# Fixed order of the first loads, b1 loaded as rows, and 40 unread transpositions ahead of TensorE's first work

## The chip, the cores and the metric

The kernel runs on one core of one Trainium2 chip. A core has five engines that each work through their own list of instructions in order: TensorE (PE, matmuls and transpositions through PSUM), VectorE (DVE), ScalarE (ACT), GpSimd (POOL) and SyncE (SP), which here only issues DMA transfers. They wait for each other and for transfers on semaphores. The metric is the device time of one execution in microseconds (us), less is better; a verdict compares medians of repeated runs.

## The reference

The program computes one layer and all its gradients. x is 2048 rows of 512. It is normalised over its rows (mean and variance), and two branches read the result: a recurrent attention with 32 heads of 128 over 64 segments of 32 rows, each preceded by 8 memory rows that the segment before has left, and an MLP with 1792 hidden units:

```python
def _B_ref(x, w1, b1, w2, b2):
    h = jnp.einsum('bsd,df->bsf', x, w1) + b1
    zero = jnp.zeros_like(h)
    r = jnp.where(h > zero, h, zero)
    h = r * r
    out = jnp.einsum('bsf,fd->bsd', h, w2) + b2
    return out
...
return x + _A_ref(xn, A_mem0, A_Wq, A_Wk, A_Wv, A_Wo, A_seg_len) + _B_ref(xn, B_w1, B_b1, B_w2, B_b2)
```

The outputs are that sum and the gradients of x, of the memory, of the four attention weights, and of w1, b1, w2, b2 for a given gradient grad_out. All inputs and outputs are bf16.

## The kernel before

The program runs stage after stage: the MLP forward together with the first half of its backward, the attention forward, the attention backward, and the weight gradients. The change touches only the start of the first stage, whose MLP matmuls the profile has up to about 220 us.

**Tiling of the first stage.** The 2048 rows are taken in eight blocks g of 256 rows. For each block, `ln(g)` normalises: ACT sums each half of the block (L1054), DVE subtracts the mean (L1059), ACT sums the squares (L1062), DVE scales (L1069), TensorE turns the result by 128 x 128 transpositions against an identity tile `ident` (L688), and DVE copies the turned block from PSUM to SBUF (L1078; the tile is PA for even blocks and xT for odd ones). `mlp_a(g)` multiplies W1 with the turned x and W2T with the turned gradient for 14 chunks of 128 hidden units (L1092, each chunk two groups of four matmuls), ACT adds b1 and applies the ReLU (L1095), DVE squares it and forms the hidden gradient (L1097, L1099), and a DVE sum over the turned gradient block gives a part of the gradient of b2 (`gb2p`, L1102). `mlp_b(g)` multiplies by W2 and by W1T.

**What has to be in place before block 0.** x block 0 (tile xN) and gradient block 0 (tile gxb, turned by TensorE into PB) come by DMA. The later gradient blocks come through a DMA that transposes (L1042, into gTb for odd blocks, PB for even ones). W1 and W2 come in four pieces each, of 4, 4, 4 and 2 chunks of 128 hidden units. W1 lies in the tile WB, W2 in a tile of its own (W in the profile). W2T and W1T are made from them by TensorE, two chunks at a time: eight transpositions into one PSUM bank, then one copy by DVE or ACT (L692, L694); that is called a turn here. b1 comes as a tile of 128 x 14 elements, b2 as one row.

**What sets the order.** Each piece of work is given to a planner with its cost, its reads and writes and, for a DMA, a time to landing. When all is given, `run()` simulates the engines and emits the instructions in the order in which the simulation has started them, by readiness and by rank (the longest chain behind a piece, plus `lift`). Once emitted, each engine keeps that order, whatever happens on the chip. The eleven large first loads, b1 and b2 were given like any other work, so the planner chose their order. That order on the SyncE queue is: W2 piece 3, a W2 piece, x block 0, a W2 piece, W1 piece 3, a W2 piece, gradient block 0, two W1 pieces, x block 1, the last W1 piece, b1, b2, the transposing load of gradient block 1, x block 2, then the first stores of normalised x (S_XN). The completion semaphores of this queue are eight that are used in turn, so that each transfer waits for the one eight places before it.

**PSUM.** The stage has two rings of four banks, "h" for the hidden chunks and "B" for the turns and the block outputs.

Of the kernel before, what the change touches and what calls it, by code (L numbers as in the profile page):

```python
# [15 lines left out]
BF16 = mybir.dt.bfloat16  # L16
F32 = mybir.dt.float32
P = 128
# [545 lines left out]
def kernel(  # L564
# [27 lines left out]
    nc = tc.nc  # L592
# [15 lines left out]
    FC = F // P  # L608
# [3 lines left out]
    xflat = A_x.flatten_outer_dims()  # L612
    gflat = grad_out.flatten_outer_dims()
# [56 lines left out]
    ident = const.tile([P, P], BF16, name="ident")  # L670
# [15 lines left out]
    def transpose_to(ps_ap, in_ap, base=0):  # L686
        k = in_ap.shape[0]
        nc.tensor.transpose(ps_ap, in_ap, ident[base:base + k, base:base + k])  # L688

    def ev(e, out, in_):  # L690
        if e == "v":
            nc.vector.tensor_copy(out, in_)  # L692
        elif e == "s":
            nc.scalar.copy(out, in_)  # L694
        else:
            nc.any.tensor_copy(out, in_)
# [22 lines left out]
    T_DMA = 0.42  # L719
# [273 lines left out]
    with tc.tile_pool(name="p0", bufs=1) as p0, \  # L993
# [4 lines left out]
        def tl(name, shape, dt=BF16):  # L998
            return p0.tile(shape, dt, name=name)

        W1 = WB[:, 0:DC * F].rearrange("p (c f) -> p c f", c=DC)
        W2T = WB[:, DC * F:2 * DC * F].rearrange("p (c f) -> p c f", c=DC)
        W2 = tl("W2", [P, FC, D])
        W1T = tl("W1T", [P, FC, D])
        b1Tb, b1T = tl("b1Tb", [P, FC]), tl("b1T", [P, FC], F32)
        b2r = tl("b2r", [1, D])
        ones_row = tl("ones_row", [1, P])
        nc.vector.memset(ones_row[:], 1.0)
# [5 lines left out]
        xN = [tl("xN%d" % z, [P, 2, D]) for z in range(3)]  # L1014
# [12 lines left out]
        gxb = [tl("gxb", [P, D], F32)] * 2  # L1027
        gN0 = gxb[0][:].bitcast(BF16).rearrange("p (c d) -> p c d", c=2)
        CUT = ((0, 4), (4, 8), (8, 12), (12, FC))
# [5 lines left out]
        sg = Stage(plan, {"h": (pp, 4), "B": (pp, 4)})  # L1035
        A = plan.add
        V = nc.vector
        R2 = lambda t, g: t[g * RB:(g + 1) * RB]
        pair = lambda t, g: R2(t, g).rearrange("(c p) d -> p c d", p=P)
# [4 lines left out]
        def ln_in(g, eng="SP"):  # L1044
            z = g % 3
            sg.dma(lambda: xN[z][:], lambda: pair(xflat, g), [], [("xN", z)], lat=3.5, eng=eng)

        def ln(g):
            z = g % 3
# [83 lines left out]
        def turn_w(u, nm):  # L1133
            bk = sg.bank("B", [P, 8, P], BF16, "ps_" + nm)
            src = W1 if nm == "W1T" else W2

            def tr(e):
                for f in range(2):
                    for dc in range(DC):
                        if nm == "W1T":  # L1140
                            transpose_to(bk()[:, DC * f + dc, :], W1[:, dc, (2 * u + f) * P:(2 * u + f + 1) * P])
                        else:
                            transpose_to(bk()[:, 2 * dc + f, :], W2[:, 2 * u + f, dc * P:(dc + 1) * P])
            A({"PE": 0.5}, tr, [(nm[:2], u // 2)], [bk.key])
            if nm == "W1T":
                out, in_ = W1T[:, 2 * u:2 * u + 2, :].rearrange("p f d -> p (f d)"), lambda: bk()[:].rearrange("p k r -> p (k r)")
            else:
                out, in_ = W2T[:, :, 2 * P * u:2 * P * (u + 1)], lambda: bk()[:].rearrange("p (c f) r -> p c (f r)", c=DC)
            A({"DVE": 0.8, "ACT": 1.1}, lambda e: ev({"DVE": "v", "ACT": "s"}[e], out, in_()), [bk.key], [(nm, u)])
# [27 lines left out]

        for g in range(NRB):
            if g == 0:
                ln_in(0)  # L1180
                for h, (f0, f1) in enumerate(CUT):
                    sg.dma(lambda f0=f0, f1=f1: W1[:, :, P * f0:P * f1],
                           lambda f0=f0, f1=f1: B_w1.rearrange("(c p) f -> p c f", p=P)[:, :, P * f0:P * f1], [], [("W1", h)], lat=4.5 + 3.0 * h)
                    if h == 0:
                        sg.dma(lambda: gN0, lambda: pair(gflat, 0), [], ["gxb"], lat=6.0)
                        sg.dma(lambda: b1Tb[:], lambda: B_b1.rearrange("(c p) -> p c", p=P), [], ["b1Tb"], lat=5.0)
                    sg.dma(lambda f0=f0, f1=f1: W2[:, f0:f1, :],
                           lambda f0=f0, f1=f1: B_w2.rearrange("(c p) d -> p c d", p=P)[:, f0:f1, :], [], [("W2", h)], lat=6.0 + 3.0 * h)
                sg.dma(lambda: b2r[:], lambda: B_b2.rearrange("(o n) -> o n", o=1), [], ["b2r"], lat=5.0)
                A({"DVE": 0.1}, lambda e: V.tensor_copy(b1T[:], b1Tb[:]), ["b1Tb"], ["b1T"])  # L1190
                ln(0)
                bk = sg.bank("B", [P, DC, RB], BF16, "ps_gT")

                def trg(e, bk=bk):
                    for k in range(2):
                        for dc in range(DC):
                            transpose_to(bk()[:, dc, k * P:(k + 1) * P], gN0[:, k, dc * P:(dc + 1) * P])
                A({"PE": 0.5}, trg, ["gxb"], [bk.key])
                A({"DVE": 0.7, "ACT": 1.05}, lambda e, bk=bk: ev({"DVE": "v", "ACT": "s"}[e], gTb[0], bk()[:]), [bk.key], [("gT", 0)])
                for u in range(FC // 2):  # L1200
                    turn_w(u, "W2T")
                ln_in(1)
                ln_in(2)
                ln(1)
            if g == 0:
                mlp_a(0)
                for u in range(FC // 2):
                    turn_w(u, "W1T")
            if g:
                mlp_a(g)  # L1210
            if g == NRB - 1:
                first_in()
            mlp_b(g)
            if g + 2 < NRB:
                ln(g + 2)
            if g + 3 < NRB:
                ln_in(g + 3)
            if g < 6:
                for h in range(2):
                    x = 2 * g + h  # L1220
                    t, dc = x // DC, x % DC
                    Wsrc = (A_Wq, A_Wk, A_Wv)[t]
                    fc = 4 + 6 * h
                    A({"POOL": 0.15}, lambda e, t=t, dc=dc, g=g, fc=fc: nc.gpsimd.tensor_copy(
                        Wqkv[t][0:1, dc, 0:1], aT[g % 2][0:1, fc, 0:1]), [("aT", g % 2, fc)], [("Wg", x)])
                    sg.dma(lambda t=t, dc=dc: Wqkv[t][:, dc, :],
                           lambda Wsrc=Wsrc, dc=dc: Wsrc[dc * P:(dc + 1) * P].rearrange("p h e -> p (h e)"),
                           [("Wg", x)], [], lat=8.0, cost=0.6, eng="POOL")
        for i in range(NI):
# [5 lines left out]
                   lat=8.0, cost=0.6, eng="POOL")  # L1235
        plan.run()

    with tc.tile_pool(name="fw", bufs=1) as fw, \
# [33 lines left out]
        for g in range(JQ):  # L1272
            h = g // 2
# [12 lines left out]
        sg = Stage(plan, {"c": (0, 4), "f": (4, 2), "m": (6, 2)}, pc.tile([P, 8, 512], F32, name="ps"), 0.9)  # L1286
        A = plan.add
        V = nc.vector
# [302 lines left out]
    if True:  # L1591
# [42 lines left out]
        sg = Stage(plan, {"c": (0, 5), "r": (5, 1), "f": (6, 2)}, pc.tile([P, 8, 512], F32, name="ps"), 1.8)  # L1634
        A = plan.add
        V = nc.vector
# [325 lines left out]
    with tc.tile_pool(name="p5b", bufs=1) as p5b, tc.tile_pool(name="p5e", bufs=1) as cs1, \  # L1962
# [142 lines left out]
```

## Time and profile before

| what | us |
|---|---|
| median of 3 runs | 2854.03 |
| lowest and highest of them | 2837.7 and 2859.14 |
| the profiled execution | 2858.51 |
| its span | 2856.7 |
| TensorE busy in the span | 2688.5 (94%) |
| VectorE busy | 1611.3 (56%) |
| ScalarE busy | 1189.5 (42%) |

Times in the profile are us from the span's start. The page has the busy time of each engine; other views of the same trace list instructions by time, with the idle time ahead of an instruction and what ended it in brackets, or the busy time of every engine in chosen stretches. PEld is TensorE's weight load, which lies beside its matmuls; SPq is the SyncE queue. Matmuls are pipelined, so for TensorE the distance from start to start says more than a duration.

### The profile page before, as it was taken

The numbers are of one execution on the slowest core, as the hardware profiler recorded it, in microseconds if no ns is written. First come the engines' busy times: TensorE is split into PE (matmuls) and PEld (weight loads), VectorE is DVE, ScalarE is ACT, GpSimd is POOL, SyncE is SP. The second block draws the span as 40 slices with busy tenths as digits, with TensorE's granted clock in tenths as the row PEclk, the third lists the DMA queues.
The fourth block names the chain that finished last, engine by engine and source line by source line (L and its number), as shares of the span: only waits on it lengthen the run. The fifth ranks groups of instructions, "written<-read, shape, count | busy, mean of one in ns | idle before, by whom it ended". The sixth has DMA issues, their size and how long they took to land. (4 is left out here: it accounts for less than half of the span.)

```text
span 2856.7 us, 113933 instructions
## 1 busy us (share of the span) xinstructions
PE 2688.5 (94%) x47469; PEld 1556.2 (54%) x47640; DVE 1611.3 (56%) x4769; ACT 1189.5 (42%) x2781; POOL 939.8 (33%) x2630
## 2 busy tenths in 40 slices
PE   8998999999999999789999999999999899999999
PEld 6664565555656555565555555555555444444444
DVE  5645667666666667566566666666666602232322
ACT  4333455455545555455555555555555400000000
POOL 1102223222322223344455554545454301111111
PEclk9999999999999999999999999999999999999999
DMA  6657768777777765368889898888888799788861
GB/s 195 213 170 200 199 196 215 207 199 200 207 203 210 200 187 165 118 149 216 221 230 240 226 236 235 232 224 232 221 233 214 207 358 298 229 255 266 253 185 43
DMA packets 557595, 606.26 MB, mean 212 GB/s; under 512 B 229925, under 2 KB 358454, under 8 KB 555030
## 3 DMA queue, kind: packets, MB, share of 16 engines
q1 hardware_dynamic: 541654, 544.09, 69.0%
q0 software_dynamic: 15424, 54.87, 5.7%
q8 instruction: 374, 6.13, 1.0%
q14 instruction: 143, 1.17, 0.2%
HBM read 290.14 MB, written 272.12 MB: 197 GB/s over the span
## 5 line engine op out<-in xcount | busy, mean ns | idle before, releaser
L802 PE MATMUL ps<-WA,PA 128*32 128x512 bf16 x6144 | 366.8, 379 | 5.5 <-DVE PA L1490 3.7
L2042 PE MATMUL ps<-WA,WB 128*128 128x512 bf16 x1505 | 330.7, 379 | 2.2 <-DVE gwo L692 0.6
L802 PEld LDWEIGHTS <-PA 128*32 128x32 bf16 x8192 | 207.3, 96 | 202.5 <-issue 12.2
L2042 PEld LDWEIGHTS <-WB 128*128 128x128 bf16 x1896 | 185.5, 98 | 224.4 <-issue 0.9
L692 DVE CAST gwo<-ps 128x512 bf16<-128x512 f32 x64 | 40.0, 683 | 398.9 <-PE ps L2042 267.2
L1660 PE MATMUL ps<-WA,dT 128*32 128x512 bf16 x4096 | 248.2, 382 | 9.7 <-DVE dT L785 8.0
L694 ACT CAST dN<-ps 128x512 bf16<-128x512 f32 x356 | 206.0, 586 | 108.9 <-PE ps L912 77.3
L694 ACT CAST gwo<-ps 128x512 bf16<-128x512 f32 x64 | 33.1, 599 | 517.2 <-PE ps L2042 357.9
L928 POOL COPY BDA<-PB 32x128 bf16<-32x128 bf16 x287 | 82.6, 288 | 413.8 <-DVE PLp L1458 266.8
L2053 POOL DMA_DIRECT2D out_dram<-gwo x96 | 71.3, 751 | 294.2 <-ACT gwo L694 263.4
L1660 PEld LDWEIGHTS <-dT 128*32 128x32 bf16 x4096 | 94.2, 97 | 125.8 <-DVE dT L785 46.8
L785 DVE STREAM_TRANSPOSE dT<-dN 128x256 f32<-128x256 f32 x256 | 109.4, 434 | 68.3 <-ACT dN L694 65.8
L934 POOL COPY BDL<-dSL 32x64 bf16<-32x64 bf16 x256 | 61.5, 240 | 255.9 <-PE ps L912 234.3
L1316 PE MATMUL ps<-WB,OT 128*32 128x256 bf16 x4096 | 134.1, 278 | 5.0 <-DVE OT L785 4.7
L802 PE MATMUL ps<-WB,PA 128*32 128x512 bf16 x2048 | 125.5, 381 | 6.6 <-issue 5.8
L1660 PE MATMUL ps<-WA,gOT 128*32 128x512 bf16 x2048 | 128.0, 380 | 1.2 <-DVE gOT L785 0.9
L934 POOL COPY BDP<-bP 32x256 bf16<-32x256 bf16 x256 | 106.7, 417 | 67.7 <-ACT BDP L928 16.3
L1542 PE MATMUL ps<-sx,anT 128*128 128x512 bf16 x352 | 116.1, 380 | 10.5 <-issue 4.3
L1316 PEld LDWEIGHTS <-OT 128*32 128x32 bf16 x4096 | 101.6, 98 | 42.2 <-DVE OT L785 32.5
L694 ACT CAST gON<-ps 128x512 bf16<-128x512 f32 x123 | 72.0, 585 | 107.7 <-PE ps L802 96.6
L928 POOL COPY BDS<-maskA 32x128 bf16<-32x128 bf16 x249 | 72.0, 289 | 128.4 <-DVE maskA L1846 122.6
L802 PE MATMUL ps<-WA,PB 128*32 128x512 bf16 x1536 | 113.4, 380 | 0.0
(320 smaller groups left out, 5753.8 us busy)
## 6 DMA issues: line engine op xcount, KB each, us to landing
S_GN<-dN SPq DMA_DIRECT2D x192, 256.0 KB
WA<-S_GN SPq DMA_DIRECT2D x160, 256.0 KB
S_K<-kN SPq DMA_DIRECT2D x64, 256.0 KB
S_Q<-qN SPq DMA_DIRECT2D x64, 256.0 KB
S_V<-vN SPq DMA_DIRECT2D x64, 256.0 KB
S_ON<-oN SPq DMA_DIRECT2D x64, 256.0 KB
bqN<-S_Q SPq DMA_DIRECT2D x64, 256.0 KB
xs<-S_Q SPq DMA_DIRECT2D x64, 256.0 KB
```

Source lines behind the costliest of these rows:

```text
L692: nc.vector.tensor_copy(out, in_)
L694: nc.scalar.copy(out, in_)
L785: self.plan.add({"DVE": 0.36}, lambda e, x=x: nc.vector.transpose(dst[:, x, :, :].rearrange("p i c r -> p (i c r)").bitcast(F32).rearrange ...
L802: nc.tensor.matmul(bk()[32 * j:32 * (j + 1), :], lhsT=win(dc), rhs=Wt(dc, c0), start=(dc == 0), stop=(dc == DC - 1), tile_position=(0, 32 ...
L928: self.plan.add({"ACT": 0.31, "DVE": 0.2, "POOL": 0.31}, lambda e, j=j: {"ACT": nc.scalar.copy, "DVE": nc.vector.tensor_copy, "POOL": nc.g ...
L934: self.plan.add(cost or {"ACT": 0.4, "DVE": 0.27, "POOL": 0.42}, lambda e, j=j: {"ACT": nc.scalar.copy, "DVE": nc.vector.tensor_copy, "POO ...
L1316: nc.tensor.matmul(bk()[32 * t:32 * (t + 1), :], lhsT=tq(OTt, i, j), rhs=Wo[:, JQ * i + j, h * HB:(h + 1) * HB], start=(i == 0 and j < 2), ...
L1542: A(pe(0.217, "f", 0.11), lambda e, c=c, z=z, x=x: nc.tensor.matmul(bks[x]()[:], lhsT=anT[x][:, c, :], rhs=sx[z][:], start=(c == 0), stop= ...
L1660: nc.tensor.matmul(bk()[32 * j:32 * (j + 1), :], lhsT=tq(XT, i, j), rhs=wtf(t, i, j), start=(first and i == 0), stop=(last and i == NI - 1 ...
L2042: nc.tensor.matmul(bks[n]()[:], lhsT=HNc[:, rc, dc * P:(dc + 1) * P], rhs=half_of(gns[y], hf), start=(y == 0), stop=(y == NRC - 1))
L2053: q.dma_start(outWs[t][dc * P:(dc + 1) * P, hf, :, j], wt[:].rearrange("p (i e) -> p i e", i=4))
```

## The change

First, the thirteen first loads and the load of x block 2 are given by a new function `first_loads()`, with a `lift` that is so high that the planner starts them ahead of anything else on SyncE, and with landing times from a running sum. The order that is emitted is x block 0, W2 piece 0, gradient block 0, x block 1, W1 piece 0, b1, W2 pieces 1 and 2, W1 piece 1, W2 piece 3, W1 pieces 2 and 3, b2, x block 2, and then the transposing load of gradient block 1. Second, b1 is loaded as 14 rows of 128 elements and turned by one TensorE transposition; DVE then copies it from PSUM. Third, 40 transpositions of the identity tile into a PSUM bank, which nothing reads, are given as TensorE's first work.

Since the planner sees other landing times, the order on the engines changes in the first rows too; from some 130 TensorE matmuls and some 220 DVE instructions on, the order is the same as before. TensorE now starts with the 40 transpositions, two turns of W2, the turn of the gradient and of b1, a turn of W2, half of x block 0, a turn of W2, the other half of x, a turn of W2, and the first MLP matmuls. On DVE the two `gb2p` sums of the blocks 0 and 1 (L1122 in the new numbering) now stand ahead of the copy of the turned x block 0 (L1098); before, both stood behind it.

```diff
-        b1Tb, b1T = tl("b1Tb", [P, FC]), tl("b1T", [P, FC], F32)
+        b1r, b1T = tl("b1r", [FC, P]), tl("b1T", [P, FC], F32)
...
+        def first_loads():
+            w1, w2 = B_w1.rearrange("(c p) f -> p c f", p=P), B_w2.rearrange("(c p) d -> p c d", p=P)
+            xl = lambda g: (lambda: xN[g][:], lambda: pair(xflat, g), ("xN", g), 0.75)
+
+            def wl(t, h):
+                f0, f1 = CUT[h]
+                kb = 0.375 * (f1 - f0)
+                if t == 1:
+                    return lambda: W1[:, :, P * f0:P * f1], lambda: w1[:, :, P * f0:P * f1], ("W1", h), kb
+                return lambda: W2[:, f0:f1, :], lambda: w2[:, f0:f1, :], ("W2", h), kb
+            todo = [xl(0), wl(2, 0), (lambda: gN0, lambda: pair(gflat, 0), "gxb", 0.75),
+                    (lambda: b1r[:], lambda: B_b1.rearrange("(c p) -> c p", p=P), "b1r", 0.05),
+                    wl(1, 0), wl(2, 1), wl(1, 1), wl(2, 2), xl(1), wl(1, 2), wl(2, 3), wl(1, 3),
+                    (lambda: b2r[:], lambda: B_b2.rearrange("(o n) -> o n", o=1), "b2r", 0.05), xl(2)]
+            land = 2.3
+            for n, (out_f, in_f, k, us) in enumerate(todo):
+                land += us
+                A({"SP": T_DMA}, lambda e, out_f=out_f, in_f=in_f: nc.sync.dma_start(out_f(), in_f()), [], [k], 1,
+                  max(land - T_DMA * (n + 1), 2.3), lift=1000.0 - n)
...
             if g == 0:
-                ln_in(0)
-                for h, (f0, f1) in enumerate(CUT):
...
-                A({"DVE": 0.1}, lambda e: V.tensor_copy(b1T[:], b1Tb[:]), ["b1Tb"], ["b1T"])
+                first_loads()
+                bk = sg.bank("h", [P, 8, P], BF16, "ps_w")
+
+                def warm(e, bk=bk):
+                    for x in range(40):
+                        transpose_to(bk()[:, x % 8, :], ident[:])
+                A({"PE": 3.0}, warm, [], [bk.key])
+                bk = sg.bank("h", [P, FC], BF16, "ps_b1")
+                A({"PE": 0.06}, lambda e, bk=bk: transpose_to(bk()[:], b1r[:]), ["b1r"], [bk.key])
+                A({"DVE": 0.1}, lambda e, bk=bk: V.tensor_copy(b1T[:], bk()[:]), [bk.key], ["b1T"])
                 ln(0)
...
                 for u in range(FC // 2):
                     turn_w(u, "W2T")
-                ln_in(1)
-                ln_in(2)
                 ln(1)
```

More of the change, by code (lines that the diff above doesn't have):

```diff
@@ L1179 @@
             if g == 0:
-                ln_in(0)
-                for h, (f0, f1) in enumerate(CUT):
[L1182 to L1190, printed above, removed]
+                first_loads()
[7 more added lines that the diff above has]
+                A({"DVE": 0.1}, lambda e, bk=bk: V.tensor_copy(b1T[:], bk()[:]), [bk.key], ["b1T"])
                 ln(0)
```

## The prediction

> **What bounds the kernel now.** The page comes first, for the engine that carries the span, then a table of stretches and the list of TensorE's instructions by time, to see where this engine stands still in the part that the diff touches.
>
> ```profile
> span 2856.7 us, 113933 instructions
> PE 2688.5 (94%) x47469; PEld 1556.2 (54%) x47640; DVE 1611.3 (56%) x4769; ACT 1189.5 (42%) x2781; POOL 939.8 (33%) x2630
> ```
>
> TensorE (PE) is busy 94% of the span; the next engine, VectorE (DVE), 56%. So time is won here only where PE stands still or runs slowly. The table of stretches gives it for the start:
>
> ```profile
> core 0: us, PE busy (x) PEld busy (x) DVE busy (x) ACT busy (x) POOL busy (x), PEclk, DMA share, GB/s
> 0.00:10.73 10.73, 0.00 (x0) 0.00 (x1) 2.51 (x19) 4.39 (x11) 6.07 (x37) 1.00 0.86 270
> 13.91:16.95 3.04, 0.01 (x1) 0.00 (x1) 0.89 (x3) 1.68 (x5) 0.00 (x0) 1.00 0.84 161
> 22.84:172.00 149.16, 148.32 (x1101) 103.09 (x1115) 90.72 (x350) 61.71 (x157) 22.21 (x36) 1.00 0.64 207
> 172.00:230.00 58.00, 57.20 (x370) 34.66 (x379) 24.67 (x103) 13.55 (x30) 7.79 (x11) 1.00 0.43 130
> ```
>
> From 22.84 us on PE is busy 148.32 of 149.16 us, and at the passage to the attention stage 57.20 of 58.00. A shift of the dense part therefore reaches the end nearly whole, and everything before it is two holes, 10.73 us and 3.04 us, and 28 + 28 transpositions. The PE list by time (start, duration, line, out<-in, count, and idle time before):
>
> ```profile
> 10.73 1.04 PE L688 MATMUL ps_W2T<-ident,W 128*128 128x128 bf16 x8 [10.73 <-DMA W<-in_B_w_dram]
> 11.56 1.06 PE L688 MATMUL ps_gT<-ident,gxb 128*128 128x128 bf16 x8
> 12.41 0.63 PE L688 MATMUL ps_xT<-ident,WB 128*128 128x128 bf16 x4
> 12.84 1.06 PE L688 MATMUL ps_W2T<-ident,W 128*128 128x128 bf16 x8
> 16.95 1.87 PE L688 MATMUL ps_W2T<-ident,W 128*128 128x128 bf16 x16 [3.04 <-ACT PB L694]
> 18.61 0.63 PE L688 MATMUL ps_xT<-ident,WB 128*128 128x128 bf16 x4
> 19.03 1.06 PE L688 MATMUL ps_W2T<-ident,W 128*128 128x128 bf16 x8
> 20.10 1.87 PE L1092 MATMUL ps_h<-PA,WB 128*128 128x256 bf16 x8
> 21.76 1.24 PE L1092 MATMUL ps_h<-PB,WB 128*128 128x256 bf16 x8
> 22.84 0.61 PE L688 MATMUL ps_W2T<-ident,W 128*128 128x128 bf16 x8
> 23.28 1.04 PE L1092 MATMUL ps_h<-PA,WB 128*128 128x256 bf16 x8
> ```
>
> The number that decides is **20.10 us**, the start of the first MLP matmuls: both programs have 5 turns of W2, the turns of x and of the gradient ahead of it, and the same PE work behind it. The second thing to see is the speed. Eight transpositions take 0.83 us start to start early on (10.73 to 11.56) and 0.44 at 22.84 (to 23.28); the first eight matmuls take 1.66 us, the next 1.08. At the later pace of 2 x 0.44 per eight, the sixteen would take 1.76 instead of 2.74 us: the cold stretch costs 0.98 us.
>
> The hole of 3.04 us comes from ScalarE (ACT), which stands in order behind a statistic of the second x block:
>
> ```profile
> 15.27 0.63 ACT L1054 ACTIVATE maskL<-xN 128x512 bf16<-128x512 bf16 x1 [4.46 <-DMA xN<-in_A_x_dram]
> 15.81 0.19 ACT L1054 ACTIVATION_READ_ACCUMULATOR maskL<-xN 128x1 f32 x1
> 15.90 0.99 ACT L694 COPY PB<-ps_gT 128x1024 bf16<-128x1024 bf16 x1
> ```
>
> **The change part by part.** *Loads.* The new order is x block 0, W2 piece 0, gradient block 0, x block 1, W1 piece 0, b1, W2 pieces 1 and 2, the rest, b2, x block 2. The second x block moves from tenth to fourth, so ACT's 4.46 us wait goes. W2 piece 0 moves to second, so the first real turns can begin some 4 us sooner. W2 piece 1, the next that PE needs, is seventh with 2304 KB up to its end (by the shapes: 256 KB for an x or gradient block, 512 for a piece of four), just as many as stood up to the sixth transfer before, whose landing is the 10.73 above. So PE has 24 transpositions still to do at about 10.7 us, 2.7 us at 0.83 per eight: 13.4. One copy later the MLP could start at about 14.2, against 20.10.
>
> *What is late next.* It does not start then. The order in which the changed program gives VectorE its work has a new wait ahead of that copy (L1098, L1078 before): the sum over gradient block 1 (L1122, L1102 before), which reads gTb, the block that a DMA transposition loads. In the kernel before that sum stands far behind:
>
> ```profile
> 18.17 0.17 DVE L1190 CAST b1T<-b1Tb 128x14 f32<-128x14 bf16 x1 [0.55 <-DMA b1Tb<-in_B_b_dram]
> ...
> 19.37 0.68 DVE L1078 COPY PA<-ps_xT 128x1024 bf16<-128x1024 bf16 x1
> ...
> 21.09 1.21 DVE L1102 TENSOR_REDUCE gb2p<-PB 128x4 f32<-128x1024 bf16 x1
> ...
> 26.60 1.21 DVE L1102 TENSOR_REDUCE gb2p<-gTb 128x4 f32<-128x1024 bf16 x1
> ```
>
> The copy started at 19.37 and PE at 20.10, 0.73 later; the sum takes 1.21 us. With L the landing of gTb, the MLP starts at L + 1.21 + 0.73 = L + 1.94. Break-even is L = 18.16. Behind that wait on VectorE stand the copy that PE waits for, a W2T copy, and the statistics of x block 1, for which ACT waits.
>
> *When gTb lands.* It is issued last of all, now behind x block 2 as well. The SyncE queue before, and the bytes moved in the first 15.0 and the first 16.0 us (two answers of the DMA view):
>
> ```profile
> 10.96 3.95 SPq L748 DMA_DIRECT2D b2r<-in_B_b_dram  x1
> 14.96 1.74 SPq L1042 DMA_TRANSPOSE gTb<-in_grad_out_dram  x1
> 16.76 0.57 SPq L748 DMA_DIRECT2D xN<-in_A_x_dram  x1
> ```
>
> ```profile
> DMA packets 4688, 4.38 MB, mean 292 GB/s; under 512 B 163, under 2 KB 4687, under 8 KB 4687
> ```
>
> ```profile
> DMA packets 6407, 4.47 MB, mean 279 GB/s; under 512 B 1799, under 2 KB 6406, under 8 KB 6406
> ```
>
> ```profile
> xN<-in_A_x_dram SPq DMA_DIRECT2D x3, 256.0 KB
> GB/s 17 1 0 0 0 0 74 119 160 215 211 152 147 88 98 123 166 287 289 306 262 262 262 328 311 377 385 393 385 385 279 115 49 49 16 0 0 0 0 0
> ```
>
> Ahead of gTb stand now the 4.47 MB and one x block, 0.26 MB: 4.73. Up to 10.73 us the table of stretches has 270 GB/s, 2.90 MB; the other 1.48 MB up to 15.0 went in 4.27 us, 0.347 MB a us. At that rate the 0.35 MB left at 15.0 take 1.0 us: 16.0. The 1600 packets of the old b1 (1799 less 163 under 512 B, almost no bytes) no longer lengthen that. The last row above is the rate in steps of 0.125 us from 16.0: after the issue ends at 16.70 come 1.5 us at 74 to 215 GB/s, the 0.26 MB of the transposition, then x and S_XN at 260 to 390. So gTb's data would move from 16.0 to 17.55. From last byte to the waiting engine: b1's packets end at 16.1 and VectorE goes on at 18.17, 2.0 us; x block 1 stood ahead of the last 0.52 MB, so its bytes were through at about 13.8, and ACT went on at 15.27, 1.5 us. L = 17.55 + 1.5 to 2.0 = 19.05 to 19.55; I take 19.3. The MLP starts at 21.24, **1.14 us later** than before, 0.9 to 1.4 by these ends.
>
> *The cold clock.* The granted clock (PEclk) is 1.00 in every row above, so only the spacing shows this. PE idles from about 13.4 to 21.24. Before, the matmuls at 20.10 followed 3.15 us of transpositions, and cost 0.98 us of slowness until about 22.1. If those transpositions helped, the new start needs the whole 5.15 us (16.95 to 22.1) at half pace, 2.58 us of loss, 1.6 more; if they didn't, 0 more. I take 0.8, the middle, as one row can't split them. The Trainium skill, TensorE: Matmul & The Clock Gate, Part 4 (PE-mode transpose), says that transpositions do not count as PE-busy for the clock gate. By it the term would be 0, the sum 1.14, and the 40 unread transpositions would be useless. The trace agrees as far as it goes: 28 in a row from 16.95 left the matmuls at 20.10 cold.
>
> *The 40 unread transpositions.* They read only ident:
>
> ```profile
> 1.21 0.29 POOL L672 TENSOR_SCALAR_AFFINE_SELECT ident<-ident 128x128 bf16<-128x128 bf16 x1
> ```
>
> From about 1.6 us, 40 x 0.104 = 4.2 us: done at 5.8, near the landing of W2 piece 0 and inside the old 10.73 us hole. They cost nothing; without that cover they would cost up to 4.2 us. *b1.* One transposition more (0.1 us) and a copy from PSUM instead of from SBUF (0.17), both in time that VectorE then spends waiting: nothing.
>
> **Sum.** 1.14 + 0.8 = +1.94 us, 0.9 to 3.0 by the bounds. The profiled execution took 2858.51 us (span 2856.7), so 2860.5 on its own account; it lies 4.5 us above the median of the three runs. On the median 2854.03: 2856.0. Those runs span 2837.7 to 2859.14, so below 1% (28.5 us) nothing can be told from no change. Everything behind the start keeps its order.
>
> **The rivals.** *Faster: the transposition overtakes the loads.* If gTb is not served behind the queue, only its issue counts. It reuses the completion semaphore of W2 piece 1, so it is issued at 10.73 or later; the first bytes came 1.8 us after the issue began (14.96 to 16.76), then 1.5, then 1.5 to 2.0: L = 15.5 to 16.0, the start at 17.7, 2.4 us earlier: -1.6 with the clock term, 2852. Were the wait missing altogether, 20.10 - 14.2 = 5.9 and up to 0.98 of warm clock: -6.9, 2847. Against both: the rate row shows the transposition's slow bytes first and those of the later x behind it, in order of issue.
>
> *Slower: the transposition starts late and lands as slowly as in later blocks.*
>
> ```profile
> 38.01 1.23 SPq L1042 DMA_TRANSPOSE PB<-in_grad_out_dram  x1
> ```
>
> ```profile
> 44.62 1.22 DVE L1102 TENSOR_REDUCE gb2p<-PB 128x4 f32<-128x1024 bf16 x1 [1.99 <-DMA PB<-in_grad_out_dram]
> ```
>
> That one took 6.6 us from issue to use. If SyncE is held back by full rings as it was at b2 (3.95 us) and issues at 14.3, L is 20.9 and the start 22.84: +2.7, and +1.6 with the full clock term, 4.3: 2858. It decides from an issue later than 11.56 (18.16 - 6.6). For it: the load; against it: in that stretch other queues moved weights and S_GT at once.
>
> *The change does nothing* (loads land in their old order whatever the issue): +0, which isn't to be told from the forecast.
>
> **How the numbers follow.** Forecast, between 0 and +3: 0.55. Faster, -1.6 to -6.9: 0.28. Slower, +4.3: 0.17. All lie within 1%: the chances of over 1% are what repeated runs could do by themselves, 0.03 faster and 0.03 slower, 0.94 within. The cases span 2847 to 2858; the three runs lay 16 below and 5 above their median, and a new median scatters by perhaps half of that whole width either way: 2842 to 2865.
>
> **What would show it.** The first MLP matmul at 21.0 to 21.5 us, VectorE's gb2p sum of gTb behind a DMA wait of some 5 us or more, PE idle for over 5 us ahead of it, cold matmuls for 2 to 5 us behind it. ACT no longer waits 4.46 us for x. I am wrong if the matmuls start at 14 to 18 us, if the dense part from there isn't the same length, or if a later stage moves by more than this start.

## The result and the profile after

| | before | after |
|---|---|---|
| median of 22 runs each, taken together, us | 2853.32 | 2858.45 |
| mean, us | 2852.5 | 2859.3 |
| lowest and highest, us | 2837.7 and 2860.66 | 2850.04 and 2870.88 |
| profiled execution and its span, us | 2858.51, 2856.7 | 2854.97, 2853.1 |

The ratio after to before is **1.0026, with an interval of 1.0015 to 1.0038**: 4 to 11 us slower, 6.7 us by the means. The forecast was 2856.0 and slower by 1.9. The sign was right and the time lies in the stated 2842 to 2865, but that range is as wide as the scatter of single runs, and the loss is about three and a half times the sum: the interval of 4 to 11 us doesn't reach down to the band of 0 to +3 that the prediction held most likely. The profiled execution of after is shorter than that of before, and one execution scatters by 5 to 6 us (the standard deviation of the 22): two single spans can't be subtracted here. What can be compared is one place of the program in both traces, where the work in between stands in the same order.

The page of after, span and TensorE:

```profile
span 2853.1 us, 114187 instructions
PE 2705.5 (95%) x47681; PEld 1564.3 (55%) x47681; DVE 1614.2 (57%) x4770; ACT 1188.0 (42%) x2780; POOL 939.7 (33%) x2630
```

TensorE's list by time in after (start, duration, line, out<-in, count, and in brackets the idle time ahead and what ended it):

```profile
1.56 4.45 PE L688 MATMUL ps_w<-ident 128*128 128x128 bf16 x40 [1.56 <-POOL ident L672]
5.80 1.39 PE L688 MATMUL ps_W2T<-ident,W 128*128 128x128 bf16 x16
7.02 0.61 PE L688 MATMUL ps_gT<-ident,gxb 128*128 128x128 bf16 x8
9.19 0.18 PE L688 MATMUL ps_b<-ident,b1r 14*128 14x14 bf16 x1 [1.56 <-DMA b1r<-in_B_b_dram]
10.48 1.03 PE L688 MATMUL ps_W2T<-ident,W 128*128 128x128 bf16 x8 [1.11 <-DMA W<-in_B_w_dram]
...
13.35 1.06 PE L688 MATMUL ps_W2T<-ident,W 128*128 128x128 bf16 x8
22.16 1.87 PE L1112 MATMUL ps_h<-PA,WB 128*128 128x256 bf16 x8 [7.75 <-DVE var_t L1084]
23.82 1.92 PE L1112 MATMUL ps_h<-PB,WB 128*128 128x256 bf16 x8
25.53 1.06 PE L688 MATMUL ps_W2T<-ident,W 128*128 128x128 bf16 x8
26.38 1.32 PE L1112 MATMUL ps_h<-PA,WB 128*128 128x256 bf16 x8
```

The turns are done at 14.4 us, and then TensorE stands still for 7.75 us. The first MLP matmuls start at 22.16, against 20.10 before. The releaser is put down to the small DVE operation that stands directly behind the copy into PA; the list of VectorE shows where the time went:

```profile
9.50 1.21 DVE L1122 TENSOR_REDUCE gb2p<-PB 128x4 f32<-128x1024 bf16 x1
...
20.29 1.22 DVE L1122 TENSOR_REDUCE gb2p<-gTb 128x4 f32<-128x1024 bf16 x1 [7.14 <-DMA gTb<-in_grad_out_dram]
21.43 0.68 DVE L1098 COPY PA<-ps_xT 128x1024 bf16<-128x1024 bf16 x1
```

This is the forecast mechanism: the sum over gradient block 1 waits 7.14 us for its transposing load, and the copy for which TensorE waits stands behind it in the same list. ScalarE's 4.46 us wait for the second x block is gone; its longest for x is now

```profile
3.56 0.63 ACT L1074 ACTIVATE maskL<-xN 128x512 bf16<-128x512 bf16 x1 [1.32 <-DMA xN<-in_A_x_dram]
```

The stretches of after, with the granted clock (PEclk) in the third column from the right:

```profile
core 0: us, PE busy (x) PEld busy (x) DVE busy (x) ACT busy (x) POOL busy (x), PEclk, DMA share, GB/s
22.16:24.84 2.68, 2.68 (x13) 1.92 (x13) 1.45 (x6) 1.10 (x2) 0.00 (x0) 0.50 0.00 0
24.84:172.00 147.16, 147.16 (x1097) 101.83 (x1095) 89.83 (x345) 60.96 (x158) 21.90 (x36) 0.99 0.62 202
```

The restart runs at a clock of 0.50, which here the records also show. For the matmuls at 20.10 in before, just as slow, the table said 1.00; the trace of before has no clock record ahead of 22.2 us, so that was a missing record and not a measured clock. From 24.84 to 172 us TensorE is busy without a gap, so the loss is carried on. The place to read it is the one transposition behind the MLP stage, ps_gb, called **the mark** from here on. Before:

```profile
228.57 0.22 PE L688 MATMUL ps_gb<-ident,gb2b 128*4 128x128 bf16 x1
```

After:

```profile
231.96 0.22 PE L688 MATMUL ps_gb<-ident,gb2b 128*4 128x128 bf16 x1
```

At the mark after is **3.39 us late**: 2.06 by the later start (22.16 - 20.10), and 1.33 by the colder clock behind it. The runs say 6.7 for the whole program. So what happens up to the mark explains about half, and something behind the mark the rest.

### The profile page after: what moved, and what is told of

It is laid out like the page before. It is cut to its first block, busy times and chain, and to the rows that moved or that the text cites. A ratio compares the mean times of both kernels' runs of the same rounds, so it can differ in the third digit from the quotient of the medians.

```text
span 2853.1 us, 114187 instructions
## 1 busy us (share of the span) xinstructions
PE 2705.5 (95%) x47681; PEld 1564.3 (55%) x47681; DVE 1614.2 (57%) x4770; ACT 1188.0 (42%) x2780; POOL 939.7 (33%) x2630
## 3 DMA queue, kind: packets, MB, share of 16 engines
q8 instruction: 374, 6.13, 0.9%
## 5 line engine op out<-in xcount | busy, mean ns | idle before, releaser
L802 PE MATMUL ps<-WA,PA 128*32 128x512 bf16 x6144 | 366.1, 379 | 5.2 <-DVE PA L1507 3.7
L802 PEld LDWEIGHTS <-PA 128*32 128x32 bf16 x8192 | 209.1, 96 | 195.0 <-DVE PA L1507 11.9
L1559 PE MATMUL ps<-sx,anT 128*128 128x512 bf16 x448 | 138.3, 381 | 2.4 <-DMA sx<-in_grad_out_dram 2.4
L802 PE MATMUL ps<-WB,PA 128*32 128x512 bf16 x2048 | 125.0, 383 | 1.9 <-issue 1.2
L802 PE MATMUL ps<-WA,PB 128*32 128x512 bf16 x1536 | 113.5, 381 | 0.0
```

The lines of the kernel that those rows point to most:

```text
L802: nc.tensor.matmul(bk()[32 * j:32 * (j + 1), :], lhsT=win(dc), rhs=Wt(dc, c0), start=(dc == 0), stop=(dc == DC - 1), tile_position=(0, 32 ...
L1559: A(pe(0.217, "f", 0.11), lambda e, c=c, z=z, x=x: nc.tensor.matmul(bks[x]()[:], lhsT=anT[x][:, c, :], rhs=sx[z][:], start=(c == 0), stop= ...
```

## The experiments

Each kernel was compared with the kernel before on the same chip. Differences of means have their standard error in parentheses; "mark" is the place of ps_gb in the kernel's profile, against 228.57 us.

**The sum late.** In the changed kernel the sums of the blocks 0 and 1 are made to wait for a piece of the same block's MLP work, and so stand behind the copy again. All else stays.

```diff
-  ..., op=ALU.add), [("gT", z)], [("gb2p", g)])
+  ..., op=ALU.add), [("gT", z)] + ([("tick", g, 1)] if g < 2 else []), [("gb2p", g)])
```

> The changed kernel, but the two gb2p sums of the gradient blocks 0 and 1 read a mark that the first MLP matmuls set, so that they can't stand ahead of the copy of the turned x block 0. If the wait of VectorE for gTb made the loss, the first MLP matmul comes at 14 to 15 us (22.16 in the changed kernel, 20.10 before), the first transposition of gb2 at the end of the MLP stage comes at 222 to 224 us (231.96 and 228.57), and the whole is 0.2 to 0.3% faster than before. If another load or the cold clock holds the start, the first MLP matmul comes after 18 us, the mark at 226 or later, and the whole is within 0.1% of before.

TensorE's list of this kernel:

```profile
5.62 1.06 PE L688 MATMUL ps_W2T<-ident,W 128*128 128x128 bf16 x16
6.52 0.61 PE L688 MATMUL ps_gT<-ident,gxb 128*128 128x128 bf16 x8
...
12.29 1.04 PE L1112 MATMUL ps_h<-PA,WB 128*128 128x256 bf16 x8
13.16 1.04 PE L1112 MATMUL ps_h<-PB,WB 128*128 128x256 bf16 x8
```

```profile
220.02 0.22 PE L688 MATMUL ps_gb<-ident,gb2b 128*4 128x128 bf16 x1
```

With the wait away the MLP starts at 12.29 us, and the mark comes 8.55 us earlier than before and 11.94 earlier than after. So the wait is what holds the start of the changed kernel. But the total did not follow, and the expected 0.2 to 0.3% did not come: 2859.01 against 2855.12, ratio 1.001 [0.9994, 1.0026], +2.0 us (2.1) by the means. Some 10 us of a gain that the trace shows at 220 us are gone at the end. That was expected by no theory, and most of what follows was made to find where it went.

**Without the 40 transpositions.** The changed kernel less the 40.

```diff
-                def warm(e, bk=bk):
-                    for x in range(40):
-                        transpose_to(bk()[:, x % 8, :], ident[:])
-                A({"PE": 3.0}, warm, [], [bk.key])
```

> The changed kernel without the 40 unread transpositions. If TensorE idles until gTb has been summed anyway, the first MLP matmul stays at 22.0 to 22.4 us and the mark at the stage's end at 231.5 to 232.5; the first turns of W2 run at 104 ns each. If the 40 transpositions keep anything warm that counts, the mark comes 1 us or more later, at 233.

One run gave 2862.89 us. VectorE's list:

```profile
18.23 1.22 DVE L1122 TENSOR_REDUCE gb2p<-gTb 128x4 f32<-128x1024 bf16 x1 [4.98 <-DMA gTb<-in_grad_out_dram]
19.37 0.68 DVE L1098 COPY PA<-ps_xT 128x1024 bf16<-128x1024 bf16 x1
```

The start, 20.10 us, and the mark, 228.94, miss the expectation: gTb is in use 2.06 us sooner than in after, though no load has changed, and the start is that of before. The bytes tell why. The rate of all transfers from 15 to 21 us in steps of 0.15 us, in after:

```profile
GB/s 311 307 304 314 311 297 323 328 282 232 196 114 49 34 20 21 17 22 263 288 301 466 369 362 355 178 7 7 7 7 14 7 27 27 14 0 0 0 0 0
```

and in the kernel without the 40:

```profile
GB/s 318 304 318 324 294 323 300 268 232 181 119 85 38 38 138 287 295 352 362 403 375 369 41 0 0 0 0 0 0 0 0 0 0 0 0 0 0 0 0 0
```

Both have the low stretch and then the block's bytes, followed by those of the S_XN store; in after they come some 0.5 us later, and then a tail of 7 to 27 GB/s runs from 18.9 to 20.2 us, where the other has nothing. The trace has sixteen semaphore updates for the landing of a block, as many as there are DMA engines: for gTb fifteen had come by 18.74 us, the last at 20.27, and VectorE went on at 20.29. Without that last one the landing would have been near 18.7. The records of single transfers also show what else there was. The block's own bytes, in pieces of 256 bytes, had all moved by 18.26. In the same stretch from 15 to 21 us, the queue q8, which carries instructions, has one transfer in after:

```profile
q8 instruction: 1, 0.02, 1.1%
```

It is of 16,384 bytes and lasts from 18.16 to 19.18 us, and the tail behind it is one piece after another, as on one engine. Without the 40, the first such transfer comes at 24.44 us. So in the profiled execution of after the last report, and with it the 2.06 us, most likely goes back to the 40 themselves: they bring this transfer forward to where it meets the block. That is an argument from two traces, no run was made to test it, and why the report came another 1.1 us behind the transfer no view shows. Taken again, with twelve runs:

> The changed kernel without the 40 transpositions, now timed. Its first MLP matmul stood at 20.10 us and its mark at 228.94, 0.4 us behind before. If the changed kernel's loss is the wait for gTb (0 to 3.4 us at the mark) plus what the 80 instructions cost later, the whole is within 0.1% of before, and 0.1 to 0.3% faster than the changed kernel. If the loss stays at 0.26%, the 40 transpositions have no part in it.

The sum stood at 18.31 us, the MLP start at 20.18, the mark at 229.17 (+0.6), the ratio was 1.0006 [0.999, 1.0023], +2.2 us (1.8). Here too the first instruction transfer comes late, at 23.84 us, and the last report of gTb at 18.29. So without the 40 the changed kernel can't be told from before: the wait on VectorE takes back what the new loads gain, and no more. Whether other executions of after have the late report stays open: it was profiled once.

**The transposing load first.** It goes to the head of the queue; the sums still stand ahead of the copy into PA:

```diff
+                if n == 4:
+                    A({"SP": 1.5}, lambda e: nc.sync.dma_start_transpose(gTb[1], R2(gflat, 1)), [], [("gT", 1)], 1, 3.5, lift=1050.0)
...
-            if g:
+            if g > 1:
```

> The changed kernel with the transposing load of gradient block 1 as the very first transfer. If transfers of this queue move in order, gTb is there at 6 to 7 us, its sum waits for little, every other load comes 1.5 to 2 us later than in the changed kernel, the first MLP matmul starts at 15.5 to 17 us and the mark comes at 224 to 226. If a transposing load is slow beside other loads wherever it stands, the sum waits until after 10 us, and the MLP starts at 18 us or later.

VectorE's and TensorE's list:

```profile
7.19 1.21 DVE L1124 TENSOR_REDUCE gb2p<-gTb 128x4 f32<-128x1024 bf16 x1
```

```profile
16.19 1.86 PE L1114 MATMUL ps_h<-PA,WB 128*128 128x256 bf16 x8
```

The sum, still ahead of the copy, no longer waits for the block, and the start comes 5.97 us earlier than in after. What costs is the late landing together with the order; the order alone costs little once the block is there. The mark is at 225.19. The one run, 2864.76 us, tells nothing at this scatter.

**The wait alone, in the kernel before.** Block 1 is loaded behind x block 2, and its sum is put ahead of the copy into PA. No transpositions, no new order of the other loads.

```diff
+            if g == 0:
+                A({"SP": 1.5}, lambda e: nc.sync.dma_start_transpose(gTb[1], R2(gflat, 1)), [], [("gT", 1)], 1, 3.5, lift=-1000.0)
+                gb2_sum(1)
-            ..., [bk.key], [("xT", g % 2)])
+            ..., [bk.key] + ([] if g else [("gb2p", 1)]), [("xT", g % 2)])
```

> The kernel before, with only the sum over gradient block 1 put ahead of the copy of the turned x block 0 on VectorE (and its load behind x block 2, as in the changed kernel). If that wait makes the loss by itself, gTb lands at 19.5 to 20.5 us, the first MLP matmul starts at 22 to 23 us, 2 to 3 us later than before, and the mark at the stage's end moves from 228.57 to 230.5 to 232. If the loss came from the new order of the loads, the MLP starts within 0.5 us of 20.10.

VectorE's list, then TensorE's:

```profile
20.25 1.22 DVE L1087 TENSOR_REDUCE gb2p<-gTb 128x4 f32<-128x1024 bf16 x1 [2.47 <-DMA gTb<-in_grad_out_dram]
...
21.91 0.68 DVE L1081 COPY PA<-ps_xT 128x1024 bf16<-128x1024 bf16 x1
```

```profile
22.64 1.03 PE L1098 MATMUL ps_h<-PA,WB 128*128 128x256 bf16 x8 [2.40 <-DVE var_t L1064]
```

The mark is at 231.78, +3.21 us against before. The wait by itself, put into the kernel before, delays the start and the stage. That the amount is nearly that of after (+3.39) is luck: the block is late here since SyncE issues it only at 16.36 us, in after it was issued at 11.35 and its last report was late. The one run gave 2858.81.

**The 40 transpositions alone.** The kernel before with the 40 put in front, and nothing else changed:

```diff
+                def warm(e, bk=bk):
+                    for x in range(40):
+                        transpose_to(bk()[:, x % 8, :], ident[:])
+                A({"PE": 3.0}, warm, [], [bk.key], lift=1000.0)
```

> The kernel before with nothing but the 40 unread transpositions ahead of TensorE's first work. The first MLP matmul stays at 20.1 us and the mark at the end of the MLP stage at 228.6 in every theory, since the transpositions end at 6 us and TensorE then idles until its loads land. If only the start counts for the whole, the time is that of before within 0.15%. If 80 more instructions on TensorE's list (another place of all later ones in its stream) cost something in the later stages, the whole is 0.15 to 0.4% slower, with the first stage as before.

TensorE's list:

```profile
1.56 4.45 PE L688 MATMUL ps_w<-ident 128*128 128x128 bf16 x40 [1.56 <-POOL ident L672]
10.48 1.03 PE L688 MATMUL ps_W2T<-ident,W 128*128 128x128 bf16 x8 [4.47 <-DMA W<-in_B_w_dram]
...
20.23 1.09 PE L1092 MATMUL ps_h<-PA,WB 128*128 128x256 bf16 x8
21.16 1.04 PE L1092 MATMUL ps_h<-PB,WB 128*128 128x256 bf16 x8
```

The 40 are done at 6.0, inside the old hole, and the mark is 0.80 us earlier than before (227.77), since the sixteen matmuls are warm sooner. All the same the total is worse: 2862.45 against 2858.36, ratio 1.0017 [1.0002, 1.0032], +4.8 us (1.9). Work that is hidden to the last instruction costs time later.

**The sum late, without the 40.** The first two edits together.

> The changed kernel with the gb2p sums put late and without the 40 transpositions. The first MLP matmul comes at 12.5 to 14.5 us, the mark at 220 to 223 (220.02 with the 40, of which the warmer clock may be 1 us). If a gain at the start reaches the end and only the 80 more instructions took it away in the run with them, the whole is 0.2 to 0.35% faster than before. If the later stages give the gain back whatever TensorE's list looks like, the whole stays within 0.1% of before.

The start is at 13.67 (with the 40 it was 12.29, and 13.74 in the second profile below), the mark at 221.56 (-7.0). And this one keeps its gain: 2853.54 against 2858.36, **ratio 0.998 [0.9965, 0.9995]**, -5.9 us (1.9). It is below before, and before is below after.

**Other numbers of transpositions.** What do 40 unread transpositions change for work that comes hundreds of us later? They are 80 TensorE instructions (a weight load and a matmul each), and everything behind them stands 80 places further on in TensorE's list. The page has a queue of transfers that carry instructions, in before and after alike in number (the share differs by a tenth of a per cent):

```profile
q8 instruction: 374, 6.13, 0.9%
```

That is 6.13 MB / 374 = 16.4 KB each; 47681 matmuls and as many weight loads by 374 are 255 instructions a transfer. The two kernels with 128 more transpositions, 256 instructions, have one transfer more:

```profile
q8 instruction: 375, 6.14, 0.9%
```

The waits of TensorE that the profile puts down to "issue" (the engine waits for nothing else that it shows) lie whole multiples of 256 instructions apart: with all recorded instructions of TensorE counted from the end of the program, its sequencer's among them, and divided by 256, all 28 of them behind 230 us leave a remainder of 88 or 89 in after. The last of them before the final stage, in five kernels (time, and in brackets the wait): before,

```profile
2216.42 1.45 PE L802 MATMUL ps<-WB,PA 128*32 128x512 bf16 x15 [1.98 <-issue]
```

after,

```profile
2215.39 0.31 PE L868 MATMUL ps<-bkLN,dSTLL 32*32 32x128 bf16 x4 [2.03 <-issue]
```

the 40 alone,

```profile
2219.22 0.26 PE L868 MATMUL ps<-dLN,dSTLL 32*32 32x128 bf16 x1 [2.04 <-issue]
```

the sum late with the 40,

```profile
2213.45 0.24 PE L868 MATMUL ps<-bkLN,dSTLL 32*32 32x128 bf16 x4 [1.82 <-issue]
```

and the sum late without them:

```profile
2214.65 1.05 PE L802 MATMUL ps<-WB,PA 128*32 128x512 bf16 x16 [2.14 <-issue]
```

With 40 the wait comes ahead of the small 32-row matmuls of L868, without ahead of a long run of L802. Counted in the matmul records from the end of the program, it lies at 3962 in the sum-late kernel without the 40 and at 4001 or 4002 in the three with them (one record is missing in one of these): 40 matmuls apart. The remainders of all 25 waits of the sum-late kernel without the 40 are 8 or 9, of all 29 with them 88 or 89: 80 instructions apart. The waits hang on the place in the list, not on the work. If so, 128 transpositions (256 instructions, a whole block) should bring the old places back. They were put in front of the kernel before in place of the 40, and 64 as well:

```diff
-                    for x in range(40):
+                    for x in range(128):
```

> The kernel before with 128 unread transpositions instead of 40: 256 more instructions on TensorE's list, as many as one of the 16384-byte instruction transfers holds at 64 bytes each, so that the later instructions stand where they stood before within such a block. The transpositions end at 10 to 11 us, so that the first turn of W2 waits up to 0.5 us; the mark stays at 227.5 to 229.5. If the place within the blocks is what costs, the issue stalls come at the instructions of the kernel before (the one near 2216 us ahead of an L802 matmul) and the whole is within 0.1% of before. If any early work or any longer list costs, the whole is 0.15% or more slower, as with 40.

> The kernel before with 64 unread transpositions: 128 more instructions, half a block of 256. The transpositions end at 6.5 to 7.5 us; the mark stays at 227.5 to 229. If the place within the blocks matters, the issue stalls come 64 matmuls earlier in the program than before, and the whole may be slower or faster than before by 0.2%, by another amount than with 40 (+0.17%). If only early work costs, it is 0.17% slower like with 40.

With 128, the ratio is 1.0002 [0.999, 1.0015], -0.2 us (1.6), mark +0.3, and the waits lie ahead of the same instructions as before. With 64: 1.001 [0.9996, 1.0023], +0.1 us (1.6) by the means, mark -0.2; the waits lie half a block, 64 matmuls, from the old places, one, at 2233.77 us, ahead of matmuls of L1881. So it isn't the number of extra instructions that costs. The sharper test is the kernel that had lost 10 us, the sum late, with 128 in place of 40, and that with 40 once more on the same chip:

> The version with both sums late, with 128 unread transpositions in place of 40, so that all later TensorE instructions move by 256 against the version without any, and not by 80. Fetch-block theory (the cost behind the first stage comes from where the later work lies in the blocks of 256 instructions): the ps_gb mark at 221 to 224 (the 128 end at about 10.4 us and hold the W2 turns back, MLP start 13.5 to 15), about -6 us at the mark, and the total follows it: -3 to -8 us. Rival (the earlier start is lost again behind the first stage, whatever the number of transpositions): the total within 2 us of before, as with 40.

> The version with both sums late and the 40 transpositions once more, as the partner of the one with 128 on the same chip. Fetch-block theory: MLP start 12.3, mark near 220, and all the same a total of 0 to +4 us against before, so 4 to 10 us above the version with 128, though its first stage ends earlier. Rival (the first result was scatter): a total of -6 to -9 us, as the mark says.

With 128:

```profile
1.56 9.30 PE L688 MATMUL ps_w<-ident 128*128 128x128 bf16 x128 [1.56 <-POOL ident L672]
10.70 1.06 PE L688 MATMUL ps_W2T<-ident,W 128*128 128x128 bf16 x16
...
15.87 1.03 PE L1112 MATMUL ps_h<-PA,WB 128*128 128x256 bf16 x8
```

```profile
2209.50 1.05 PE L802 MATMUL ps<-WB,PA 128*32 128x512 bf16 x16 [2.43 <-issue]
```

The last wait is ahead of the same 16 matmuls of L802 as without any transpositions. The 128 hold the real turns back, the start is at 15.87 (later than the 13.5 to 15 expected) and the mark at 223.34 (-5.2). The total is 2854.85 against 2856.83, ratio 0.9992 [0.9979, 1.0004], -3.1 us (1.5). With 40 on the same chip the mark was at 221.98 (-6.6), 1.4 us earlier, and the total 2859.96, ratio 1.0006 [0.9988, 1.0024], +0.9 us (2.3). Neither interval excludes 1, and the two means differ by 4.0 us (2.3): this pair alone isn't proof. All kernels with repeated runs together:

| kernel | unread | mark, us | total, us | behind the mark |
|---|---|---|---|---|
| after | 40 | +3.4 | +6.7 (1.7) | +3.3 |
| the 40 alone | 40 | -0.8 | +4.8 (1.9) | +5.6 |
| sum late | 40 | -8.6 | +2.0 (2.1) | +10.6 |
| sum late, again | 40 | -6.6 | +0.9 (2.3) | +7.5 |
| 64 alone | 64 | -0.2 | +0.1 (1.6) | +0.3 |
| 128 alone | 128 | +0.3 | -0.2 (1.6) | -0.5 |
| sum late, 128 | 128 | -5.2 | -3.1 (1.5) | +2.1 |
| after without the 40 | 0 | +0.6 | +2.2 (1.8) | +1.6 |
| sum late, none | 0 | -7.0 | -5.9 (1.9) | +1.1 |
| another order (below) | 0 | -6.4 | -5.2 (1.8) | +1.2 |

The four kernels with 40 lose 3.3 to 10.6 us behind the mark, 6.8 in the mean; the six others -0.5 to 2.1, in the mean 1.0. Each row has a standard error of some 2 us in its total, and its mark is that of one execution (two of the same kernel had 220.02 and 221.98); rows of one chip share their runs of before. Even so the groups stand apart. That these 40 transpositions cost about 6 us in later stages, give or take two, is shown. That the waits for "issue" move with the place in the blocks of 256 instructions is shown too. That this is what costs the 6 us fits the kernels with 128, but 64 move the waits as well and cost nothing, and which waits make up the 6 us is not shown. TensorE's waits for "issue" from 230 us to the end, by line (us in total, times, longest), before:

```profile
PE ps L802 <- issue: 6.8, 9, 2.0
PE ps L1542 <- issue: 4.3, 27, 0.2
PE ps L912 <- issue: 2.5, 3, 1.9
...
PE ps L868 <- issue: 0.7, 1, 0.7
```

and after:

```profile
PE ps L912 <- issue: 8.7, 10, 2.9
PE ps L868 <- issue: 4.5, 4, 2.0
...
PE ps L802 <- issue: 2.0, 4, 0.7
```

They move from the long matmuls of L802 to the attention backward's small ones of L912 and L868 (there a wait may also delay the other engines' chain, which is an argument and was not tried). All the "issue" rows of that stretch add up to 21.7 us before and 22.1 after, or 17.4 and 22.1 without the 27 small ones of L1542, which stand where the trace of before lacks records (352 of these matmuls against 448 in after). With only the waits at the block places counted, the five traces with 40 have 19.9 to 22.0 us, the nine others 12.2 to 21.1, 20.7 and 17.6 in the mean: the direct sum gives some 3 us, not 6, and some traces lack records.

Two other ways for the place to cost time stand in the traces and were not tried. A wait of about 2 us can also halve the clock behind it: in before the wait that ends at 2216.42 us goes with a clock record of 0.50 from 2216.9 to 2220.3, in after that of 2215.39 with one from 2214.9 to 2218.3. In these profiled executions that doesn't tell the groups apart, since before, after and the 40 alone each have 34.1 us at 0.50 between 230 us and the end of the work. And each instruction transfer takes about 1 us of one DMA engine, so that a block that lands in that time can be reported late, as gTb was in after.

**Another order of the loads.** To the best version, b1 to second place, W2's pieces ahead of W1's, x block 1 eighth (gN0 and b1r stand for the entries of gradient block 0 and of b1):

```diff
-            todo = [xl(0), wl(2, 0), gN0, b1r, wl(1, 0), wl(2, 1), wl(1, 1), wl(2, 2), xl(1), ...
+            todo = [xl(0), b1r, wl(2, 0), gN0, wl(2, 1), wl(1, 0), wl(2, 2), xl(1), wl(1, 1), ...
...
-                  max(land - T_DMA * (n + 1), 2.3), lift=1000.0 - n)
+                  max(land - T_DMA * (n + 1), 2.3), lift=20000.0 - 1000.0 * n)
```

> The changed kernel without the 40 transpositions, with the gb2p sums put late, and with b1 second and W2 piece 1 ahead of W1 piece 0 and x block 1 in the queue. The first MLP matmul comes at 11 to 13 us (13.67 without the new order), the mark at 219 to 221 (221.56), the whole 0.2 to 0.4% faster than before. If the later stages give a gain at the start back, it stays within 0.1%.

The start was 14.76 us, not 11 to 13: the planner, which saw other landing times, put a turn of W1 and half of x block 0 behind later turns of W2. Mark 222.19, ratio 0.9985 [0.9971, 0.9999], -5.2 us (1.8): as good as the version without the 40 above, and no better.

## Why the prediction was right in sign and short in size

- **What bounds the start.** Right. VectorE's sum over gTb, not the loads that the change puts in front, sets the MLP start. The sum moved away (12.29 us), the load moved forward (16.19) and the wait put into the kernel before (+3.21 at the mark) show it from three sides. But by itself this wait only brings the start back to that of before: without the 40 it is 20.10 and 20.18, and the total +2.2 us (1.8). The start of after came later than 20.10, as forecast, but by a late report that the forecast had not in it: the sign at the start was in part luck.
- **The formula L + 1.94.** Right within 0.1 us: 20.29 + 1.94 = 22.23 for 22.16 measured; without the 40, 18.23 + 1.94 = 20.17 for 20.10. The start that the prediction gave without the wait, 14.2, was late: 12.29 and 13.74 with the 40, 13.67 without; with the 40 part of the turns ran warm, the rest of the difference was not taken apart.
- **L = 19.3 (19.05 to 19.55).** Off by 1.0 in after, and by as much on the other side without the 40 (18.23, 18.31). What failed is the last step, one lag of 1.5 to 2.0 us behind the last byte (and 16.0 + 1.5 is 17.5, not 17.55). Without the 40 the block's last byte moved at 17.74 and 17.78 and VectorE went on 0.5 us behind it. In after it moved at 18.26, and the last of sixteen reports came 2.0 us behind it, 1.5 behind the other fifteen. At 18.23 the start is that of before, so this term can be anything from 0 to the 2.06 that was seen. The range given was too narrow by 0.8 below and 0.7 above.
- **The cold clock, 0.8 (0 to 1.6).** Mis-sized: 1.33 in after, inside the bounds. The 1.00 that it read in the rows ahead of 22.2 us was no measured clock, as said above. After a pause of 7.75 us the matmuls of 22.16 took 0.21 us each until about 27.0, against 0.109 warm (0.87 for eight in the sum-late kernel). The Trainium skill, TensorE: Matmul & The Clock Gate, Part 4 (PE-mode transpose), which says that transpositions don't count as busy for the clock gate, does not hold here: with 40 transpositions as TensorE's only work the next 16 took 0.90 us (5.62 to 6.52), 0.056 each, where the 40 had taken 0.1; and 128 of them left the turns at 10.70 warm. The clock records say the same: with the 40 alone it is 1.00 from 6.7 us on, when they are all that TensorE has done. The measurement decides. The prediction read the cold matmuls at 20.10 behind 28 transpositions as agreement; with the 40 alone the same 28 start at 17.01, and the matmuls behind them are warm from the second on, at 20.39, those of before from 22.2. So transpositions bring the clock up, but the moment differs by some 2 us from execution to execution.
- **"They cost nothing" and "Everything behind the start keeps its order".** This is the step that failed. The 40 are hidden where they run, and the order behind them is kept, but their 80 instructions move the rest of TensorE's list, and the kernels with 40 lose some 6 us behind the mark. In the profiled execution of after they most likely also made the block late, 2.06 us at the start. In the sum it stood as zero, with the price of a missing cover (4.2 us) as the only alternative; the measured cost has nothing to do with cover.
- **The sum.** +1.94 (0.9 to 3.0) against 3.39 at the mark and 6.7 in all. The prediction had named "a later stage moves by more than this start" as a sign of being wrong, and that is what the total shows.
- **The rivals.** Faster fell: the transposing load didn't overtake. Slower (+4.3) came nearer to the size at the mark, by another way: SyncE began the issue at 11.35 us, before the rival's point of 11.56, and not at 14.3; it was the issue itself that took long, 4.24 us against 1.23 later on, as the row below shows; what held SyncE in it (the prediction says full rings) no view shows. Its 6.6 us from issue to use fit the kernel without the 40 (11.51 to 18.23, 6.7) better than the forecast's sum of bytes did; in after it was 8.9. That the change does nothing fell as well.

SyncE's list of after:

```profile
10.57 0.74 SPq L1065 DMA_DIRECT2D xN<-in_A_x_dram  x1
11.35 4.24 SPq L1042 DMA_TRANSPOSE gTb<-in_grad_out_dram  x1
```

## What to carry to other kernels

When a planner rewrites the order of a stage, look on each in-order engine for work that nobody needs soon but that reads the last transfer in the queue: it holds everything behind it, and one added dependency that puts it back is worth more than the order of the loads (here 8 to 12 us at the end of the stage). Instructions that hide perfectly in a hole still shift every later instruction of their engine, and the transfers that bring those instructions in; in a program of tens of thousands of them, compare totals with and without such filling, and with other counts, before it is called free. And a gain that one trace shows at the end of a stage is not yet a gain of the program: it has to be found again in the medians.

## What the runs showed of the hardware that was not expected

TensorE's waits for "issue", up to 2.9 us long, lie at places that go with the position in the instruction list in steps of 256 instructions; 80 more instructions moved them by 40 matmuls and cost about 6 us in 2855, 128 and 256 more cost nothing that could be measured.

Transpositions alone bring the clock up, in the sum-late kernel after 3.8 us (at 0.107 us each from 1.56 to about 5.4, then 0.056), and short waits may or may not bring it down again: in one execution of the sum-late kernel TensorE paused for 1.40, 0.73 and 0.66 us and was warm at 12.29, in the other for 1.86, 0.73 and 0.76 us and the turns at 12.06 ran at half pace (16 in 1.68 us).

One DMA engine of sixteen reported 1.5 us behind the others in the profiled execution of after, and with it the whole block, while an instruction transfer of 16,384 bytes was under way for 1.0 us. That is no single case: of the landings in the fourteen traces whose sixteen reports can be told apart, the last report came over 0.5 us behind the fifteenth in 188 of 299 where such a transfer was under way in the half us before, and in 283 of 1444 where none was.
